# The last three attention chunks in shared runs: one run of sketches, one run of numerators

## The chip, the cores and the metric

The kernel runs on one core of a Trainium2 chip. The metric is the device time of one execution in microseconds (us); lower is better. Five engines work in parallel, each through its own list of instructions in order: TensorE (PE in the profile, its weight loads PEld), VectorE (DVE), ScalarE (ACT), GpSimd (POOL) and SyncE (SP), which issues transfers.

## The reference: what is computed

A sketched attention and an MLP with an exact gelu follow each other. Everything is float32.

```python
# q, k, v: (batch 4, heads 4, 1088 tokens, 32); S1, S2: (8, 32)
phi(x) = outer(S1 @ x, S2 @ x), flattened to 64        # for each token
kv  = sum over tokens of phi(k) x v                    # 64 x 32 for each batch and head
z   = sum over tokens of phi(k)                        # 64
att = (phi(q) @ kv) / (phi(q) @ z + 1e-6)
x   = att as (4352 tokens, 128)                        # heads side by side
h   = x @ w_in                                         # (4352, 2048)
out = (0.5 * h * (1 + erf(h / sqrt(2)))) @ w_out       # (4352, 128)
```

## The kernel before

**Chunks.** The tokens of each batch are cut into two chunks of 512 (`CW`); with four batches that makes `NMAIN` = 8 main chunks, numbered 0 to 7. The last 64 tokens of all four batches together form the remainder, chunk 8 (`NMAIN`), 256 tokens wide. Chunks 2b and 2b + 1 belong to batch b.

**Steps.** The MLP sets the pace. `steps` lists the pairs (chunk, fi), 16 values of fi for each chunk: one step is one block of 128 hidden channels. In each step `hidden` (L692) multiplies the chunk's tokens `xT[n]` by a piece of w_in, ScalarE takes the gelu (L699), and the products with w_out (`two_products`, L776) of earlier steps follow. From chunk 2 on the output product is done with sums of token halves that GpSimd makes (`token_sums`, L741 to L744); `drain` (L791 to L797, with ScalarE's copies L788 and L789) takes its accumulators, and `store` combines, transposes (L838) and sends the result through SP (L853). Chunk n starts at step 16n. The order is written out by hand: `at(t, f)` puts a piece of other work into `slots[t]`, behind the hidden product of step t and ahead of the output products of that step. The last lines tie each engine to the order of the text.

**The attention work in the slots.** For each chunk n from 2 on:

- `query_turn` (L519): VectorE transposes the queries into `qT[n]`.
- `query_sketch` (L568): TensorE multiplies them by `S_abc[b]`, which holds S1, S1 weighted with batch b's z, and S2. The output goes to the first half of each of two PSUM banks.
- `query_outer` (L580 to L603): VectorE transposes the sketch into the other half of the same banks, sums the denominators, takes reciprocals, builds the features divided by them, and transposes those into `qp[n]`.
- `attend` (L617): TensorE multiplies `qp[n]` by `kz[b]`, which gives the numerators, already divided; ScalarE copies them to `xT[n]` (L623).

Between batches there are also, ahead of the first chunk of batch b: `z_sum` (L428 with `k_s` and `ones`), the sum of key features; `fold_z` (L483, L485, L486), in which VectorE weights the sketch with z and writes it into `S_abc[b]`; `kv_sum` (L428 with `k_p` and `v`); `take_kv` (L453), ScalarE's copy of kv to `kv_T[b]`; and `turn_kv` (L458, L459), which turns it into `kz[b]`.

**Runs of small products.** `hidden` and `two_products` use all 128 rows of the array with 64 columns each (128\*64 in the profile). `query_sketch` and `attend` use 64 rows with 32 columns (64\*32), and `kv_product` 128 rows with 32 columns. Where such products follow each other without a hidden product in between, the text calls that a run. Before the change the runs towards the end are, by the step in whose slot they stand:

| step | run |
|---|---|
| 79 | z of batch 3, kv of batch 3, numerators of chunk 5, sketch of chunk 6 |
| 81 | `turn_kv` for batch 3 (128\*64) |
| 95 | numerators of chunk 6, sketch of chunk 7 |
| 111 | numerators of chunk 7, sketch of chunk 8 |
| 127 | numerators of chunk 8 |

Each `query_outer` stands right behind the sketch that it works on. Numerators of a chunk are made in the slot just ahead of its first hidden product.

**Banks.** `work_banks()` gives a tile of two PSUM banks from a pool of two such tiles (`w_ps`). Each of z, kv with numerators, and sketch takes a tile of its own in the run at step 79: `z_sum` a `work_bank()`, `kv_and_attend` a `work_banks()`, `query_sketch` a `work_banks()`. Buffers that matter: `qT`, `q_pT` two each, `xT` three, `q_f` one.

Of the kernel before, what the change touches and what calls it, by code (L numbers as in the profile page):

```python
# [8 lines left out]
FP = mybir.dt.float32  # L9
# [7 lines left out]
def kernel(  # L17
# [21 lines left out]
    F = R * R  # L39
    d_model = out.shape[1]  # L40
    d_ff = moe_w_in.shape[1]
    NF = d_ff // 128
# [5 lines left out]
    CW = JC * 128  # L48
# [4 lines left out]
    NMAIN = B * NCH  # L53
# [7 lines left out]
    att = ctx.enter_context(tc.tile_pool(name="att", bufs=2))  # L61
# [5 lines left out]
    def work_banks():  # L67

        return wps.tile([128, 2, CW], FP, name="w_ps")

    def work_bank():
        return work_banks()[:, 0]
# [159 lines left out]
    ones = big.tile([128, D], FP, name="ones")  # L232
# [173 lines left out]
    k_s = {}  # L406
# [19 lines left out]
    def kv_product(ps, lhsT, features, h, part, start=False, stop=False):  # L426

        pe.matmul(ps[h * D:(h + 1) * D, part * F:(part + 1) * F], lhsT=lhsT, rhs=features, start=start, stop=stop,  # L428
                  skip_group_check=True)

    def kv_sum(b, ps):


        for i in range(J):
            for h in range(H):
                kv_product(ps, main["v", b][:, h, i, :], k_p[b][h // 2][:, i, h % 2], h, 0, start=i == 0)
        for h in range(H):
            kv_product(ps, v_rem_aug[b][:, h, :], flat(k_p_rem[b % 2][:, h]), h, 0, stop=True)

    def z_sum(b):  # L440

        held["z"] = work_bank()
        for h in range(H):
            kv_product(held["z"], ones, k_s[b][:, h], h, 0, start=True, stop=True)

    def fold_z(b):
        sketch_of_z(b, held["z"], 0)
# [3 lines left out]
    def take_kv(b, ps):  # L451
        kv_T[b] = att.tile([128, F], FP, name="kv_T")
        act.copy(out=kv_T[b], in_=ps[:, :F])  # L453

    def turn_kv(b, banks):

        for rows in (slice(0, 64), slice(64, 128)):
            pe.matmul(banks[rows, 1, :128], lhsT=kv_T[b], rhs=ident, start=True, stop=True)  # L458
        act.copy(out=kz[b], in_=banks[:, 1, :128])  # L459
# [48 lines left out]
    qT, qp, xT = {}, {}, {}  # L508
# [15 lines left out]
    def expand_products(n):  # L524


        W = width[n]
        for i in range(2):
            B_of[n, i] = work_banks()
        for s in range(2):  # L530
            for g in range(G):
                for c in range(NP):
                    rows = slice(g * D, (g + 1) * D)
                    pe.matmul(B_of[n, g // 2][c * F:(c + 1) * F, g % 2, s * W // 2:(s + 1) * W // 2],  # L534
                              lhsT=Srep[rows, s].rearrange("p i j -> p (i j)"),
# [7 lines left out]
    def expand_multiply(n, i):  # L543
        W = width[n]
        a, b = (t.rearrange("f g (r x) -> f g r x", r=2) for t in (A[i][:, :, :W // 2], B_of[n, i][:, :, W // 2:W]))
# [8 lines left out]

    sketched = {}

    def query_sketch(n, ps=None):

        ps = work_banks() if ps is None else ps
        W = width[n]  # L560
        m = 1 if n < NMAIN else B // 2
        N = W // 2 // m
        for s in range(2):
            for i in range(m):
                for fh in range(2):
                    for c in range(NP):
                        rows, q4 = slice(c * 64, (c + 1) * 64), 2 * s + fh
                        pe.matmul(ps[q4 * 32:(q4 + 1) * 32, c, i * N:(i + 1) * N],  # L568
                                  lhsT=S_abc[batch_of(n, s, i)][rows, fh].rearrange("p r x -> p (r x)"),
                                  rhs=qT[n].rearrange("p h j t -> p (h j t)")[rows, (s * m + i) * N:(s * m + i + 1) * N],  # L570
                                  start=True, stop=True)
        sketched[n] = ps

    def query_outer(n):

        W = width[n]
        K, H2 = W // 16, W // 2
        ps = sketched.pop(n)
        tok = ps[:, :, CW // 2:CW // 2 + H2]
        dve.transpose(out=tok, in_=ps[:, :, :H2])  # L580
        x = tok.rearrange("p c (k x) -> p c k x", x=2 * R)
        a, b = x[:, :, :, 0:4], x[:, :, :, 8:16]
        m = att.tile([128, 32, 4], FP, name="q_ac")[:, :K]
        den = att.tile([128, 32], FP, name="q_den")[:, :K]
        by_c = lambda t: t.rearrange("p (c k) i -> p c k i", c=NP)
        dve.tensor_copy(out=by_c(m), in_=x[:, :, :, 4:8])
        dve.tensor_mul(out=by_c(m), in0=a, in1=by_c(m))
        part = ps[:, 0, :K]
        dve.tensor_reduce(out=part, in_=m, axis=mybir.AxisListType.X, op=AX.add)
        for g in range(4):  # L590
            dve.tensor_reduce(out=den[(g ^ 1) * 32:((g ^ 1) + 1) * 32], in_=m[g * 32:(g + 1) * 32], axis=mybir.AxisListType.X,
                              op=AX.add)
        dve.scalar_tensor_tensor(out=den, in0=part, scalar=1e-6, in1=den, op0=AX.add, op1=AX.add)
        dve.reciprocal(out=den, in_=den)
        dve.tensor_mul(out=by_c(m), in0=a,
                       in1=den.rearrange("p (c k) -> p c k", c=NP)[:, :, :, None].broadcast_to([128, NP, K // 2, 4]))
        feat = att.tile([128, 2 * CW], FP, name="q_f", bufs=1)[:, :2 * W]
        qp[n] = att.tile([128, 2, CW], FP, name="q_pT")
        for c in range(NP):
            dve.tensor_mul(out=feat[:, c * W:(c + 1) * W].rearrange("p (k i j) -> p k i j", i=4, j=R),  # L600
                           in0=by_c(m)[:, c, :, :, None].broadcast_to([128, K // 2, 4, R]),
                           in1=b[:, c, :, None, :].broadcast_to([128, K // 2, 4, R]))
        dve.transpose(out=qp[n].rearrange("f r x -> f (r x)")[:, :2 * W], in_=feat)  # L603

    def attend(n, banks=None):


        W = width[n]
        m = 1 if n < NMAIN else B // 2
        banks = work_banks() if banks is None else banks  # L610
        f = qp[n].rearrange("f r x -> f (r x)")[:, :2 * W].rearrange("f (c i n r t) -> f c i n r t", c=NP, i=m, r=2, t=32)
        N = W // 2 // m
        for i in range(m):
            for s in range(2):
                rows, b = slice(s * 64, (s + 1) * 64), batch_of(n, s, i)
                for h in range(H):
                    pe.matmul(banks[h * D:(h + 1) * D, s, i * N:(i + 1) * N],  # L617
                              lhsT=(kz[b] if b else kz_first)[rows, h * D:(h + 1) * D],
                              rhs=f[rows, h // 2, i, :, h % 2], start=True, stop=True)
        xT[n] = att.tile([128, CW], FP, name="xT", bufs=3)  # L620
        to = xT[n][:, :W]
        to = to.rearrange("p (s x) -> p s x", s=2) if m == 1 else to.rearrange("p (s t i) -> p s i t", s=2, i=m)
        act.copy(out=to, in_=banks[:, :, :W // 2] if m == 1 else banks[:, :, :W // 2].rearrange("p s (i t) -> p s i t", i=m))  # L623
# [253 lines left out]
    banks = [out_bank(), out_bank()]  # L877
# [59 lines left out]
    def at(t, f, *a):  # L937
        slots[t].append(lambda: f(*a))
# [40 lines left out]
    held = {}  # L979

    def sketch_and_attend(n):
# [2 lines left out]
        query_sketch(n, ps)  # L984
        attend(n - 1, ps[:, :, CW // 2:])

    def turn_keys_rem(pair):
        held["rem"] = work_bank()
        key_turn_rem(pair, held["rem"], by_act)
# [46 lines left out]
    for n in range(3, NCHUNK):  # L1036

        t = (n - 1) * NF
        b = (n + 1) // 2 if n % 2 else n // 2
        keys = n % 2 and b < B  # L1040
        if n > 3:
            at(t - 6, query_turn, n)
        if keys:
            at(t - 1, sketch_and_attend, n)
            at(t - 1, features_of_all, b)
        else:
            if n % 2 == 0 and b < B:
                at(t - 1, z_sum, b)
                at(t - 1, fold_z, b)
                at(t - 1, kv_and_attend, b, n - 1)  # L1050
                at(t + 1, lambda b=b: turn_kv(b, held["kv"]))
            else:
                at(t - 1, attend, n - 1)
            at(t - 1, query_sketch, n)
        at(t - 1, query_outer, n)
        if keys:
            for r in range(2):
                at(t - 3 if n > 3 else t - 4, key_turn_blocks, b, r)

        if n == NMAIN:  # L1060
            at(t + 15, attend, n)
        if keys:
            at(t + 5 + (n == NCH + 1), outer_of_all, b)
            at(t + 5 + (n == NCH + 1), add_tokens, b)
            at(t + 8, widen_v_rem, b)
            if b == 2:
                at(t + 10, turn_first_kv)
# [5 lines left out]
    for t, (n, fi) in enumerate(steps):  # L1073
# [13 lines left out]
        elif fi % NB == NB - 1:  # L1087
            b = fi // NB
# [11 lines left out]
    for t in range(len(steps) + LAG):  # L1100
        if t < 4:
# [9 lines left out]
            if t == 3:  # L1111
                banks = work_banks()
# [23 lines left out]
        if t < len(steps):  # L1136
            n, fi = steps[t]
            hidden(n, fi, by_halves=t >= 18 and (n < NMAIN or fi < 5))
        if t < len(steps) and steps[t][0] < NMAIN and steps[t][1] % NB == NB - 1:
            n, b = steps[t][0], steps[t][1] // NB  # L1140
# [50 lines left out]
```

## Time and profile before

| | us |
|---|---|
| median of 3 runs | 259.96 (259.6 to 260.07) |
| the profiled execution's own time | 259.86 |
| its span, first to last instruction | 258.0 |
| PE busy | 253.8 |
| POOL busy | 163.8 |
| DVE busy | 150.6 |
| ACT busy | 115.0 |
| mean granted TensorE clock | 1.000 |

The span leaves out 1.9 us of the profiled execution's own time. Durations of single instructions come from this one execution. Ends of matmuls are modelled, and a matmul's duration holds its way through the array, so starts say more than durations where matmuls follow each other closely. "Idle before" in brackets is the time in which the engine did nothing ahead of the instruction, and behind it stands who ended it.

### The profile page before, as it was taken

The page shows a single profiled execution, that of the slowest core. Times are in us where ns is not written, and L with a number is a line of the kernel's source. Part 1 is how long each engine was busy: PE and PEld are TensorE (multiplying, and loading weights), DVE is VectorE, ACT ScalarE, POOL GpSimd, SP SyncE. Part 2 cuts the span into 40 slices and gives each one's busy share as a digit, 9 for nine tenths or more (in the row PEclk, how much of TensorE's full clock was granted, in tenths as well). Part 3 has the DMA queues.
Part 4 walks back from the last instruction along what each step waited for, and adds up shares of the span by engine and source line. Part 5 has one row for each costly group of instructions (what it writes and reads, how often), then busy time and mean ns, then how long its engine had stood idle before and what let it go on. Part 6 is the DMA issues. An engine that isn't in the chain of part 4 may idle for free.

```text
span 258.0 us, 5758 instructions
## 1 busy us (share of the span) xinstructions
PE 253.8 (98%) x2331; PEld 134.8 (52%) x2331; DVE 150.6 (58%) x312; ACT 115.0 (45%) x222; POOL 163.8 (63%) x173
## 2 busy tenths in 40 slices
PE   8999999999999999999999999999999999999995
PEld 7856444355444545454444455454445444445794
DVE  2896879969698996580278958530565043600330
ACT  4675767433535333533335334533353335334442
POOL 3504016799968777587758784867778776877200
PEclk9999999999999999999999999999999999999999
DMA  6479748820000101101000020020001100010020
GB/s 203 141 211 366 193 94 216 218 54 10 3 0 15 29 1 23 20 13 31 3 0 3 0 35 9 3 41 0 3 0 24 20 4 0 13 31 0 3 41 20
DMA packets 29594, 13.48 MB, mean 52 GB/s; under 512 B 21888, under 2 KB 27776, under 8 KB 29568
## 3 DMA queue, kind: packets, MB, share of 16 engines
q1 hardware_dynamic: 29392, 13.05, 20.3%
q8 instruction: 18, 0.29, 0.4%
q10 hardware_dynamic: 176, 0.07, 0.1%
q14 instruction: 8, 0.07, 0.1%
HBM read 10.88 MB, written 2.23 MB: 51 GB/s over the span
## 4 chain that ended last, share of the span: by engine, by line
PE 98%; ACT 0%; issue 0%
PE h_ps L692 45%; PE o_ps L776 33%; PE o_ps L827 5%; PE w_ps L824 3%; PE w_ps L428 1%; PE w_ps L859 1%; PE w_ps L617 1%; PE w_ps L568 1%; PE o_ps L417 1%; PE w_ps L534 1%; PE h_ps L706 1%; PE w_ps L947 1%; PE h_ps L333 1%; PE w_ps L635 0%; PE w_ps L333 0%; PE h_ps L373 0%
## 5 line engine op out<-in xcount | busy, mean ns | idle before, releaser
L692 PE MATMUL h_ps<-xT,w_in 128*64 128x512 f32 (+3 forms) x514 | 136.9, 576 | 0.0
L699 ACT ACTIVATE block<-h_ps 128x512 f32<-128x512 f32 (+1 forms) x128 | 73.0, 571 | 118.5 <-PE h_ps L692 118.1
L692 PEld LDWEIGHTS h_ps<-xT,w_in 128*64 128x64 f32 (+1 forms) x514 | 41.9, 142 | 30.6 <-issue 11.6
L776 PE MATMUL o_ps<-block,w_out 128*64 128x256 f32 x224 | 57.5, 379 | 0.0
L741 POOL TENSOR_TENSOR bits_low<-block 128x512 f32<-128x512 f32 x28 | 35.8, 1280 | 27.7 <-ACT block L699 27.7
L776 PEld LDWEIGHTS o_ps<-block,w_out 128*64 128x64 f32 x224 | 30.5, 137 | 38.0 <-issue 27.2
L742 POOL TENSOR_TENSOR bits_a<-block 128x512 f32<-128x512 f32 x28 | 35.8, 1277 | 12.0 <-ACT block L699 12.0
L743 POOL TENSOR_TENSOR bits_e<-bits_a,block 128x512 f32<-128x512 f32 x28 | 36.1, 1289 | 2.2
L744 POOL TENSOR_TENSOR bits_m<-block,bits_e 128x512 f32<-128x512 f32 x28 | 35.8, 1278 | 2.2
L580 DVE STREAM_TRANSPOSE w_ps<-w_ps 128x512 f32<-128x512 f32 (+1 forms) x7 | 4.9, 693 | 42.2 <-PE w_ps L568 29.5
L776 PE MATMUL o_ps<-bits_a,small 128*64 128x256 f32 x112 | 28.8, 379 | 0.0
L776 PE MATMUL o_ps<-block,small 128*64 128x256 f32 x112 | 28.8, 379 | 0.0
L776 PE MATMUL o_ps<-bits_low,small 128*64 128x256 f32 x112 | 28.8, 379 | 0.0
L776 PE MATMUL o_ps<-bits_m,w_out 128*64 128x256 f32 x112 | 28.7, 379 | 0.0
L776 PEld LDWEIGHTS o_ps<-block,small 128*64 128x64 f32 x112 | 15.2, 137 | 17.3 <-issue 10.2
L791 DVE COPY sums<-o_ps 64x256 f32<-64x256 f32 x8 | 3.3, 417 | 35.0 <-PE o_ps L776 35.0
L776 PE MATMUL o_ps<-bits_e,small 128*64 128x256 f32 x112 | 17.2, 384 | 0.0
L827 PE MATMUL o_ps<-g,w_out 128*128 128x512 f32 (+1 forms) x34 | 16.5, 572 | 0.0
L776 PEld LDWEIGHTS o_ps<-bits_m,w_out 128*64 128x64 f32 x112 | 15.3, 137 | 0.0
L776 PEld LDWEIGHTS o_ps<-bits_a,small 128*64 128x64 f32 x112 | 15.2, 137 | 0.0
L776 PEld LDWEIGHTS o_ps<-bits_low,small 128*64 128x64 f32 x112 | 15.2, 137 | 0.0
L776 PEld LDWEIGHTS o_ps<-bits_e,small 128*64 128x64 f32 x112 | 7.5, 136 | 10.5 <-issue 8.2
(182 smaller groups left out, 302.2 us busy)
## 6 DMA issues: line engine op xcount, KB each, us to landing
block<-in_moe_w_in_dram SPq DMA_DIRECT2D x3, 512.0 KB, 6.6
block<-in_moe_w_out_dram SPq DMA_DIRECT2D x3, 512.0 KB, 11.9
k<-in_k_dram SPq DMA_DIRECT2D x12, 128.0 KB, 2.8
v<-in_v_dram SPq DMA_DIRECT2D x12, 128.0 KB, 3.1
q<-in_q_dram SPq DMA_DIRECT2D x24, 64.0 KB, 2.2
out_dram<-oT SPq DMA_DIRECT2D x21, 64.0 KB, 2.2
k<-in_k_dram SPq DMA_DIRECT2D x2, 256.0 KB, 2.9
q<-in_q_dram SPq DMA_DIRECT2D x2, 256.0 KB, 4.0
```

The costliest lines, as they stand in the source:

```text
L333: pe.transpose(ps[:, i * 128:(i + 1) * 128], in_=s, identity=ident)
L580: dve.transpose(out=tok, in_=ps[:, :, :H2])
L692: pe.matmul(ps[rows, :W], lhsT=w[:, rows], rhs=xT[n][:, :W], start=True, stop=True)
L699: act.activation(out=g_of[n, fi][:, :W], in_=ps[:, :W], func=ACT.Gelu)
L741: pool.tensor_sub(out=s[3], in0=a11, in1=a21)
L742: pool.tensor_add(out=s[1], in0=a21, in1=a22)
L743: pool.tensor_sub(out=s[2], in0=s[1], in1=a11)
L744: pool.tensor_sub(out=s[4], in0=a12, in1=s[2])
L776: pe.matmul(acc[n][bank][half * 64:(half + 1) * 64, col:col + HW], lhsT=fixed, rhs=moving, start=opens and e == 0 and name in "4715", stop ...
L791: dve.tensor_copy(out=N[lo, 0, one], in_=a0[lo, one])
L824: pe.matmul(o_of[n][i][:, :128], lhsT=g[:, i * 128:(i + 1) * 128], rhs=w_tile(w_out_sb, fi), start=first, stop=final)
L827: pe.matmul(o_of[n][:, cols], lhsT=w_tile(w_out_sb, fi), rhs=g[:, cols], start=first, stop=final)
```

## The change

The sketches of chunks 6, 7 and 8 are made in one run, in the slot of step 79, behind the kv of batch 3 and the numerators of chunk 5. The numerators of chunks 6, 7 and 8 are made in one run, in the slot of step 95. The runs at steps 111 and 127 fall away. `turn_kv` for batch 3 moves from step 81 to step 91. The queries of all three chunks are transposed in the slot of step 74 (before: 74, 90 and 106). `query_outer` of chunk 8 stands right behind the sketches, that of chunk 6 in the slot of step 86, that of chunk 7 in that of step 89.

To find room in the two tiles, the pieces share them. `first` holds z (bank 0, second half), kv (bank 1, second half), then the sketch of chunk 6 (first halves) and that of chunk 8 (in the second halves, from column 320 on). `other` holds the numerators of chunk 5 (first halves) and the sketch of chunk 7 (second halves). Each `query_outer` is told where to put its transposed sketch (`tok`). In the second run, chunks 6 and 7 use the two halves of one tile, and chunk 8 another tile. The features of chunk 8 get a buffer of their own, `q_pT_rem`.

```diff
+    def z_sum_into(b, ps):
         for h in range(H):
-            kv_product(held["z"], ones, k_s[b][:, h], h, 0, start=True, stop=True)
+            kv_product(ps, ones, k_s[b][:, h], h, 0, start=True, stop=True)
...
-    def query_sketch(n, ps=None):
+    def query_sketch(n, ps=None, tok=None):
 
         ps = work_banks() if ps is None else ps
         W = width[n]
+        tok = ps[:, :, CW // 2:] if tok is None else tok
...
-        sketched[n] = ps
+        sketched[n] = ps, tok
...
-        ps = sketched.pop(n)
-        tok = ps[:, :, CW // 2:CW // 2 + H2]
+        ps, tok = sketched.pop(n)
+        tok = tok[:, :, :H2]
         dve.transpose(out=tok, in_=ps[:, :, :H2])
...
-        qp[n] = att.tile([128, 2, CW], FP, name="q_pT")
+        qp[n] = att.tile([128, 2, W], FP, name="q_pT" if n < NMAIN else "q_pT_rem", bufs=2 if n < NMAIN else 1)
...
+    def last_sketches(b):
+
+        first, other = work_banks(), work_banks()
+        held["z"] = first[:, 0, CW // 2:]
+        z_sum_into(b, held["z"])
+        fold_z(b)
+        kv_sum(b, first[:, 1, CW // 2:])
+        attend(NMAIN - 3, other)
+        take_kv(b, first[:, 1, CW // 2:])
+        query_sketch(NMAIN - 2, first)
+        query_sketch(NMAIN - 1, other[:, :, CW // 2:], other)
+        query_sketch(NMAIN, first[:, :, CW // 2 + F:], other)
+        query_outer(NMAIN)
+
+    def last_attends():
+
+        banks = work_banks()
+        attend(NMAIN - 2, banks)
+        attend(NMAIN - 1, banks[:, :, CW // 2:])
+        attend(NMAIN)
...
+        if n == NMAIN - 2:
+            for m in (n, n + 1, NMAIN):
+                at(t - 6, query_turn, m)
+            at(t - 1, last_sketches, b)
+            for i in range(2):
+                at(t + 6 + 3 * i, query_outer, n + i)
+            at(t + 11, lambda b=b: turn_kv(b, work_banks()))
+            at(t + NF - 1, last_attends)
+        if n >= NMAIN - 2:
+            continue
...
-        if n == NMAIN:
-            at(t + 15, attend, n)
```

More of the change, by code (lines that the diff above doesn't have):

```diff
@@ L985, in sketch_and_attend @@
         attend(n - 1, ps[:, :, CW // 2:])
+    def last_sketches(b):
+        first, other = work_banks(), work_banks()
+        held["z"] = first[:, 0, CW // 2:]
+        z_sum_into(b, held["z"])
+        fold_z(b)
[11 more added lines that the diff above has]
+        attend(NMAIN)
     def turn_keys_rem(pair):
```

## The prediction

> **What bounds the kernel now.** I read the page first: busy times and the chain of work that ended last.
>
> ```profile
> PE 253.8 (98%) x2331; PEld 134.8 (52%) x2331; DVE 150.6 (58%) x312; ACT 115.0 (45%) x222; POOL 163.8 (63%) x173
> ...
> PE 98%; ACT 0%; issue 0%
> ```
>
> TensorE (PE) is busy for 98% of the span and is 98% of the chain; no other engine is above 63%. So what counts is time added to or taken from TensorE's own line, and every moment in which it stands still in the steady part moves the end by as much. I therefore read the timeline around the attention runs. Columns: start, duration, engine, line, operation. First the run ahead of chunk 5, with batch 3's kv:
>
> ```profile
> 153.25 0.32 PE L428 MATMUL w_ps<-k_s,ones 128*32 128x64 f32 x8
> ...
> 153.39 1.08 PE L428 MATMUL w_ps<-k_p,v 128*32 128x64 f32 x64
> 153.64 0.23 DVE L483 TENSOR_TENSOR z_s<-w_ps,sT 128x64 f32<-128x64 f32 x1 [2.34 <-PE w_ps L428]
> 153.90 0.23 DVE L485 TENSOR_REDUCE w_ps<-z_s 128x8 f32<-128x64 f32 x1
> 154.16 0.17 DVE L486 TENSOR_TENSOR S_abc<-w_ps,own_r 128x16 f32<-128x16 f32 x1
> ...
> 154.50 0.66 PE L617 MATMUL w_ps<-q_pT,kz 64*32 64x256 f32 x16
> ...
> 154.96 0.64 PE L568 MATMUL w_ps<-qT,S_abc 64*32 64x256 f32 x16
> 155.27 0.58 ACT L623 COPY xT<-w_ps 128x512 f32<-128x512 f32 x1 [1.31 <-PE w_ps L617]
> 155.53 0.65 PE L776 MATMUL o_ps<-bits_e,small 128*64 128x256 f32 x4
> ...
> 155.76 0.22 ACT L453 COPY kv_T<-w_ps 128x64 f32<-128x64 f32 x1
> 155.91 0.25 PEld L692 LDWEIGHTS h_ps<-xT,w_in 128*64 128x64 f32 x4 [0.19 <-ACT xT L623]
> 156.01 1.03 PE L692 MATMUL h_ps<-xT,w_in 128*64 128x512 f32 x4
> ```
>
> Here TensorE never waits: it goes from z (L428, k_s) to kv at once while VectorE folds z (until 154.33) beside it, and from the numerators (L617) to the sketch (L568) at once while ScalarE copies xT and kv_T (until 155.98) beside it. Then the run ahead of chunk 6, which ends with the sketch of chunk 7:
>
> ```profile
> 180.76 1.03 PE L692 MATMUL h_ps<-xT,w_in 128*64 128x512 f32 x4
> 181.72 0.18 PEld L617 LDWEIGHTS w_ps<-q_pT,kz 64*32 64x32 f32 x16 [0.81 <-issue]
> 181.72 0.66 PE L617 MATMUL w_ps<-q_pT,kz 64*32 64x256 f32 x16
> ...
> 182.17 0.64 PE L568 MATMUL w_ps<-qT,S_abc 64*32 64x256 f32 x16
> 182.49 0.58 ACT L623 COPY xT<-w_ps 128x512 f32<-128x512 f32 x1
> 182.74 0.20 PEld L776 LDWEIGHTS o_ps<-bits_e,small 128*64 128x64 f32 x4 [0.41 <-issue]
> ...
> 183.22 1.03 PE L692 MATMUL h_ps<-xT,w_in 128*64 128x512 f32 x4
> ```
>
> Durations of matmuls include their way through the array, so I work with starts. A step of hidden products takes 0.86 us where the steps follow each other, so the one at 180.76 is issued by 181.62; the run starts 0.10 later. Numerators take 0.45, the sketch 0.43 (the rate of the other 256-column groups), so it is done at 182.60; the next products start 0.14 later, and their four take 0.48 instead of the usual 0.43. A run on 64-row tiles thus costs 0.10 + 0.14 + 0.05 = 0.29 us beside its own products.
>
> **What the Trainium skill says.** "TensorEngine Tiling (Array Packing)", Key Properties: a change of tiling mode drains TensorE. The trace agrees: both gaps stand where 128\*64 turns into 64\*32 and back. "PSUM — Partial Sum Buffer", PSUM bank collisions raise a hardware error: two engines that touch one bank in the same quadrant need an order between them, also at different addresses. The trace before neither shows nor denies it, as TensorE and the reader keep to different tiles there wherever that matters; for waits B and C below it gives the reason. For A it gives none (z and kv lie in the two banks of one tile), and I take the wait from the built program. The same page, Engine vs sequencer instructions: matmuls start and end in program order, so one that waits holds all behind it. "TensorE: Matmul & The Clock Gate", What's actually happening: about 3.4 us of idleness lower the clock. The waits below are near 1 us each; the clock before is 1.00 throughout, and I count nothing for it.
>
> **The change part by part.**
>
> Removed: two runs of their own, ahead of chunks 7 and 8. Their products stay (numerators of chunk 7 and of the remainder, sketches of chunk 7 and of the remainder, at the same size), but ride in runs that exist anyway. Gain 2 x 0.29 = 0.58 us on TensorE, all of it on the path.
>
> Added, wait A: z and kv now lie in one tile, `first`. In the built program kv's first product gains a wait for the last step of `fold_z` (the S_abc write). All of kv's products (64 + 8 rows in the trace), and everything behind them, queue behind it. z's first product starts at 153.25; the fold ends at 154.16 + 0.17 = 154.33. How fast a release is, the run ahead of chunk 2 shows, where TensorE did wait for such a write: L486 ends at 56.04 + 0.17 = 56.21, and L568 starts at 56.36, 0.15 later. So kv starts at 154.48 instead of 153.39: **+1.09**.
>
> Added, wait B: the sketch of chunk 6 goes into `first` too, and waits for ScalarE's copy of kv_T out of it, which is queued behind the copy of chunk 5's xT. Numerators to start of the xT copy 155.27 − 154.50 = 0.77; to the end of kv_T 155.98 − 155.27 = 0.71; release 0.15 (xT ends at 183.07, and L692 starts at 183.22). Together 1.63 after the numerators' start, where the sketch started 0.46 after it: **+1.17**. Behind it stand all three sketches and chunk 5's first hidden step. The sketches of chunks 7 and 8 add no wait.
>
> Added, wait C: ahead of chunk 6 the numerators of chunks 6 and 7 go into halves of one tile, `banks`, and those of chunk 7 wait for the xT copy of chunk 6: 0.77 + 0.58 + 0.15 = 1.50 after the first start instead of 0.45: **+1.05**. The remainder's numerators have a tile of their own and no wait more.
>
> Moved at no cost, and under what cover. Three query transposes now follow each other on VectorE ahead of z (0.71 + 0.45 more): it was idle for 2.34 us before L483, so 1.2 us are left. The remainder's `query_outer` (about 4.4 us, L580 at 209.84 to L603's end at 214.27) follows the sketches at once, in an idle stretch of VectorE before chunk 4's drain. `query_outer` of chunks 6 and 7 follow that drain, 6.4 us each (155.72 to 162.13): with the drain's end 11.8 us after chunk 5's first hidden step (167.78 − 156.01), they end at 18.2 and 24.6, and the numerators start at 25.7. `turn_kv` is later (its two products 0.22 in both places) and needs VectorE's last read of `first`, at 16.9; its place is at 18.9. Chunk 4's combine, transpose and four output DMAs on SP then come some 11 us later than before, and are needed by no one before chunk 5's drain at 35.6; the orders of SP and POOL are unchanged. ScalarE copies xT three times in a row (1.6 us in all) where it has a second of idleness per hidden step; the gelu of chunk 6's first step comes behind them, as its product does. If the cover of the two `query_outer` fails, TensorE waits for VectorE in place of C.
>
> Sum: 1.09 + 1.17 + 1.05 − 0.58 = **+2.73 us** against the profiled execution's own 259.86, which stands 0.10 under the median of the runs: 262.6.
>
> Bounds: the three waits appear nowhere in the trace before. From below each is what the reader alone takes: A 0.23 + 0.23 + 0.17 = 0.63, B 0.58, C 0.58, together 1.8 with no way between the engines, net +1.2. From above, 0.3 more for each release than I take, net +3.6. I take the sums worked out, since each of their terms is a distance seen in this trace. A gain from waiting is excluded: nothing else bounds TensorE here.
>
> **The rivals.**
>
> *Clean merge (faster).* The waits end before TensorE gets there, and only the 0.58 is left: 259.3 us. For it: the order of the text puts work between each pair. Against it: at all three places the work between is none or shorter than the reader's. It decides once the three waits together stay under 0.58 us; one xT copy alone takes that.
>
> *Waits in part covered.* One of them is no stop, or two are half as long: 261.4 us. For it: A and B lie in one run, and a late TensorE may find some of its partners done. Against it: each starts only when the product before it has ended.
>
> *VectorE becomes late.* The two `query_outer` ends come behind the numerators of chunk 7: the cover is 26.2 − 24.6 = 1.6 us, or 2.6 with wait C. If VectorE falls 3.6 us behind there, the end moves by 1 more: 263.6. Against it: the same `query_outer` takes 6.4 us at 155.7 and at 182.9.
>
> **How the numbers follow.** Forecast 0.82, covered in part 0.09, VectorE late 0.06, clean merge 0.03. The time is the forecast's, 262.6. The range 261.4 to 263.5 holds the forecast with an error of about 0.3 for each wait, and reaches to the second case and nearly the third. A measurement can tell 0.2% (0.5 us) from no change: faster 0.03, same 0.02, slower 0.95.
>
> **What would show it right or wrong.** In the timeline after: an idle of about 1.1 us ahead of the first k_p product ended by VectorE, one of about 1.2 ahead of the sketch of chunk 6 ended by ScalarE's kv_T, one of about 1.0 between the numerators of chunks 6 and 7 ended by xT; between the last hidden step of chunks 6 and 7 and the next products no gap; TensorE's busy time nearly unchanged. No idle at those places, or one ahead of numerators ended by VectorE, would prove it wrong.

## The result and the profile after

The changed kernel takes 262.72 us (median of 4 runs, 262.19 to 262.73) against 259.83 us for the kernel before (4 runs, 259.6 to 260.07): a ratio of 1.0101, 95% interval 1.0085 to 1.0117. It is slower by 2.9 us going by the medians, by 2.6 us going by the ratio; the prediction said 262.6 us and slower.

The page of the changed kernel, busy times:

```profile
PE 253.9 (97%) x2331; PEld 135.1 (52%) x2331; DVE 151.0 (58%) x312; ACT 115.1 (44%) x222; POOL 163.5 (63%) x173
```

The span went from 258.0 to 260.9 us and TensorE's busy time stayed (253.8 to 253.9): it does as much as before and stands still longer. The timeline says where. Most line numbers are three or four higher than before (L692 is now L696, L568 L572, L617 L621, L623 L627, L776 L780). The first run, step 79, in the changed kernel (start, duration, engine, line, operation; in brackets the idle before and who ended it):

```profile
153.46 0.32 PE L428 MATMUL w_ps<-k_s,ones 128*32 128x64 f32 x8
...
154.37 0.17 DVE L489 TENSOR_TENSOR S_abc<-w_ps,own_r 128x16 f32<-128x16 f32 x1
...
154.60 1.10 PE L428 MATMUL w_ps<-k_p,v 128*32 128x64 f32 x64 [0.82 <-DVE S_abc L489]
...
155.74 0.66 PE L621 MATMUL w_ps<-q_pT,kz 64*32 64x256 f32 x16
156.51 0.59 ACT L627 COPY xT<-w_ps 128x512 f32<-128x512 f32 x1 [2.34 <-PE w_ps L621]
...
157.00 0.22 ACT L456 COPY kv_T<-w_ps 128x64 f32<-128x64 f32 x1
...
157.27 1.10 PE L572 MATMUL w_ps<-qT,S_abc 64*32 64x256 f32 x32 [0.86 <-ACT kv_T L456]
...
158.16 0.63 PE L572 MATMUL w_ps<-qT_rem,S_abc 64*32 64x64 f32 x32
158.72 0.20 PEld L780 LDWEIGHTS o_ps<-bits_e,small 128*64 128x64 f32 x4
...
159.20 1.03 PE L696 MATMUL h_ps<-xT,w_in 128*64 128x512 f32 x4
```

Waits A and B are there, each ended by the instruction that the prediction named. Read the starts: from z to kv it was 0.14 us (153.25 to 153.39) and is 1.14 (153.46 to 154.60); from the numerators to the sketch it was 0.46 and is 1.53 (155.74 to 157.27). The bracketed idle is smaller than the loss, because it counts only after the modelled end of the matmuls before. Then the second run, step 95:

```profile
183.95 1.03 PE L696 MATMUL h_ps<-xT,w_in 128*64 128x512 f32 x4
...
184.91 0.66 PE L621 MATMUL w_ps<-q_pT,kz 64*32 64x256 f32 x16
...
185.68 0.59 ACT L627 COPY xT<-w_ps 128x512 f32<-128x512 f32 x1
...
186.32 0.67 PE L621 MATMUL w_ps<-q_pT,kz 64*32 64x256 f32 x16 [0.75 <-ACT xT L627]
...
186.77 0.24 PE L621 MATMUL w_ps<-q_pT_rem,kz_first 64*32 64x64 f32 x4
...
187.29 0.20 PEld L780 LDWEIGHTS o_ps<-bits_e,small 128*64 128x64 f32 x4
...
187.77 1.03 PE L696 MATMUL h_ps<-xT,w_in 128*64 128x512 f32 x4
```

Wait C: the numerators of chunk 7 start 1.41 us after those of chunk 6, where 0.45 would do. And where a run fell away, the end of chunk 6:

```profile
212.30 1.03 PE L696 MATMUL h_ps<-xT,w_in 128*64 128x512 f32 x4
...
213.16 0.60 PE L780 MATMUL o_ps<-bits_e,small 128*64 128x256 f32 x4
```

The products follow the hidden step after 0.86 us, with no gap. The table gives the stages around the four places, in us between starts. Each begins with the last hidden product of the chunk before:

| stage | before | after | difference |
|---|---|---|---|
| run ahead of chunk 5 (to its first hidden product) | 3.72 | 6.69 | +2.97 |
| run ahead of chunk 6 | 2.46 | 3.82 | +1.36 |
| ahead of chunk 7 (here no run is left) | 2.47 | 1.29 | −1.18 |
| ahead of chunk 8 (no run left; to the second group of output products) | 1.82 | 1.29 | −0.53 |
| sum | | | **+2.62** |

From the start of the first of these to the last end the traces give the same +2.62 (152.29 to 236.57; 152.51 to 239.41). So nothing is lost or won between these stages. The changed kernel's profile is already 0.2 us later at 31 us, long before anything of the change, which makes up the rest of the spans' 2.9.

### The profile page after: what moved, and what is told of

Read it like the earlier page. It is cut to its first block, busy times and chain, and to the rows that moved or that the text cites. A ratio compares the mean times of both kernels' runs of the same rounds, so it can differ in the third digit from the quotient of the medians.

```text
span 260.9 us, 5759 instructions
## 1 busy us (share of the span) xinstructions
PE 253.9 (97%) x2331; PEld 135.1 (52%) x2331; DVE 151.0 (58%) x312; ACT 115.1 (44%) x222; POOL 163.5 (63%) x173
## 4 chain that ended last, share of the span: by engine, by line
PE 97%; ACT 1%; issue 0%; DVE 0%
PE h_ps L696 44%; PE o_ps L780 33%; PE o_ps L831 5%; PE w_ps L828 3%; PE w_ps L428 2%; PE w_ps L621 1%; PE w_ps L572 1%; PE w_ps L863 1%; PE o_ps L417 1%; PE w_ps L537 1%; PE h_ps L710 1%; PE w_ps L951 1%; PE h_ps L333 0%; ACT xT L627 0%; PE w_ps L639 0%
## 5 line engine op out<-in xcount | busy, mean ns | idle before, releaser
L696 PE MATMUL h_ps<-xT,w_in 128*64 128x512 f32 (+3 forms) x514 | 136.9, 576 | 0.0
L696 PEld LDWEIGHTS h_ps<-xT,w_in 128*64 128x64 f32 (+1 forms) x514 | 41.9, 143 | 30.5 <-issue 11.6
L780 PE MATMUL o_ps<-block,w_out 128*64 128x256 f32 x224 | 57.5, 379 | 0.0
L780 PEld LDWEIGHTS o_ps<-block,w_out 128*64 128x64 f32 x224 | 30.5, 137 | 38.1 <-issue 27.5
L780 PE MATMUL o_ps<-bits_a,small 128*64 128x256 f32 x112 | 28.8, 380 | 0.0
L780 PE MATMUL o_ps<-bits_low,small 128*64 128x256 f32 x112 | 28.8, 380 | 0.0
L780 PE MATMUL o_ps<-block,small 128*64 128x256 f32 x112 | 28.8, 379 | 0.0
L780 PE MATMUL o_ps<-bits_m,w_out 128*64 128x256 f32 x112 | 28.7, 379 | 0.0
L780 PEld LDWEIGHTS o_ps<-block,small 128*64 128x64 f32 x112 | 15.2, 137 | 17.9 <-issue 10.8
L780 PE MATMUL o_ps<-bits_e,small 128*64 128x256 f32 x112 | 17.1, 383 | 0.0
L780 PEld LDWEIGHTS o_ps<-bits_m,w_out 128*64 128x64 f32 x112 | 15.3, 137 | 0.0
L780 PEld LDWEIGHTS o_ps<-bits_a,small 128*64 128x64 f32 x112 | 15.2, 137 | 0.0
L780 PEld LDWEIGHTS o_ps<-bits_low,small 128*64 128x64 f32 x112 | 15.2, 137 | 0.0
L780 PEld LDWEIGHTS o_ps<-bits_e,small 128*64 128x64 f32 x112 | 7.6, 137 | 10.3 <-issue 8.4
```

The source lines that it names most:

```text
L696: pe.matmul(ps[rows, :W], lhsT=w[:, rows], rhs=xT[n][:, :W], start=True, stop=True)
L780: pe.matmul(acc[n][bank][half * 64:(half + 1) * 64, col:col + HW], lhsT=fixed, rhs=moving, start=opens and e == 0 and name in "4715", stop ...
```

## Experiments

The theory: the loss is the three waits, and they come from pieces that share a tile of two banks; the shared runs themselves gain. The rivals: VectorE's new order makes the loss; a run less gains nothing; a lifted wait only moves to the next product. All ratios are to the kernel before on the same chip. For e1 to e4 the us are worked out from the ratio (by it the changed kernel is at +2.6), for e5 to e8 from the medians; the two differ by at most 0.3. "The stretch" is the time in a trace from the first start in the table to the first hidden product behind its last stage.

**e1: z in the other tile.** Wait A alone is lifted.

```diff
-        held["z"] = first[:, 0, CW // 2:]
+        held["z"] = other[:, 0, CW // 2:]
```

> The changed kernel with z in the tile `other` instead of `first`, so that kv shares no tile with what VectorE still reads. If the waits make the loss (theory): wait A, 1.00 us in the trace of the changed kernel, goes and nothing takes its place, since the numerators of chunk 5, which now wait for the fold, start 1.25 us after z and the fold is released 1.14 us after it: 1.0 us under the changed kernel, so about +1.9 us over the kernel before; the first kv product starts 0.14 us after z. If the loss comes from VectorE's new order (rival): nothing changes, +2.9 us. If the run as a whole is late for another reason, the idle moves to the numerators: +2.9 us.

Measured: 261.74 us, ratio 1.0066 (1.0053 to 1.0079), +1.7 us. The trace has kv 0.14 us behind z again:

```profile
153.52 0.32 PE L428 MATMUL w_ps<-k_s,ones 128*32 128x64 f32 x8
...
153.66 1.08 PE L428 MATMUL w_ps<-k_p,v 128*32 128x64 f32 x64
...
154.78 0.66 PE L621 MATMUL w_ps<-q_pT,kz 64*32 64x256 f32 x16
```

The numerators of chunk 5, which now share a tile with z, come 1.26 us after it and don't wait. The stage ahead of chunk 5 takes 5.67 us (152.56 to 158.23), 1.02 less than in the changed kernel. Waits B and C stand as in the changed kernel.

**e2: kv copied first, sketches in the order 6, 8, 7.** Wait B alone.

```diff
+        take_kv(b, first[:, 1, CW // 2:])
         attend(NMAIN - 3, other)
-        take_kv(b, first[:, 1, CW // 2:])
         query_sketch(NMAIN - 2, first)
+        query_sketch(NMAIN, first[:, :, CW // 2 + F:], other)
         query_sketch(NMAIN - 1, other[:, :, CW // 2:], other)
-        query_sketch(NMAIN, first[:, :, CW // 2 + F:], other)
```

> The changed kernel with ScalarE's copy of kv ahead of the numerators of chunk 5, and the sketches in the order 6, 8, 7. Theory: the copy of kv_T is over 0.36 us after the numerators' start, before TensorE comes to the sketch of chunk 6 at 0.46; chunk 8's sketch lies in the same tile and needs no more; chunk 7's waits for the xT copy, over 1.41 us after the numerators' start, where TensorE comes at 1.31: wait B falls from 1.07 to 0.1 us, so about +1.9 us over the kernel before. Rival (ScalarE or VectorE is late as such): the idle stays at about 1 us ahead of some sketch, +2.9 us.

Measured: 261.93 us, ratio 1.0067 (1.0054 to 1.0080), +1.7 us. The timeline of e2, the same columns:

```profile
155.84 0.66 PE L621 MATMUL w_ps<-q_pT,kz 64*32 64x256 f32 x16
156.01 0.21 ACT L456 COPY kv_T<-w_ps 128x64 f32<-128x64 f32 x1 [1.74 <-PE w_ps L428]
...
156.29 0.65 PE L572 MATMUL w_ps<-qT,S_abc 64*32 64x256 f32 x16
...
156.61 0.59 ACT L627 COPY xT<-w_ps 128x512 f32<-128x512 f32 x1 [0.39 <-PE w_ps L621]
156.73 0.64 PE L572 MATMUL w_ps<-qT_rem,S_abc 64*32 64x64 f32 x32
157.25 0.67 PE L572 MATMUL w_ps<-qT,S_abc 64*32 64x256 f32 x16
```

The kv copy now ends (156.22) before TensorE comes to the sketch, and the two sketches that need only it cover the xT copy: 0.52 us from the second to the third sketch instead of 0.42, so 0.10 of wait is left of 1.07.

**e3: the xT copies last.** `attend` is split into its products and its copy; wait C alone.

```diff
-        attend(NMAIN - 2, banks)
-        attend(NMAIN - 1, banks[:, :, CW // 2:])
-        attend(NMAIN)
+        numerators(NMAIN - 2, banks)
+        numerators(NMAIN - 1, banks[:, :, CW // 2:])
+        rest = numerators(NMAIN)
+        take_x(NMAIN - 2, banks)
+        take_x(NMAIN - 1, banks[:, :, CW // 2:])
+        take_x(NMAIN, rest)
```

> The changed kernel with the numerators of chunks 6, 7 and 8 issued first and the three xT copies behind them, so that no product waits for a copy. Theory: wait C (0.96 us) goes; chunk 6's first hidden product needs its xT by about 1.9 us after the run's start, and it is there by 1.9 at the latest: about +1.9 us over the kernel before, at most 0.1 more. Rival (the copy is late for the hidden product instead): the wait moves to the first hidden product of chunk 6 and the time stays at +2.9 us.

Measured: 261.48 us, ratio 1.0057 (1.0044 to 1.0069), +1.5 us (+1.1 to +1.8), a little better than expected; the stage ahead of chunk 6 takes 2.84 us (184.35 to 187.19), 0.98 less than in the changed kernel. In e3's timeline the copies start only behind the products of both chunks in the tile, and still end in time:

```profile
185.31 1.09 PE L624 MATMUL w_ps<-q_pT,kz 64*32 64x256 f32 x32
...
186.51 1.38 ACT L636 COPY xT<-w_ps 128x512 f32<-128x512 f32 x3 [0.49 <-PE w_ps L624]
...
186.71 0.65 PE L789 MATMUL o_ps<-bits_e,small 128*64 128x256 f32 x4
187.15 0.20 PEld L705 LDWEIGHTS h_ps<-xT,w_in 128*64 128x64 f32 x4 [0.24 <-ACT xT L636]
187.19 1.03 PE L705 MATMUL h_ps<-xT,w_in 128*64 128x512 f32 x4
```

**e4: the three edits together.**

> The three edits together (z in the other tile, kv copied first with sketches 6, 8, 7, the xT copies last). Theory: only the gain of two runs less is left, 0.58 us, less 0.1 us of rest wait and 0.14 us that the remainder's numerators take more in the shared run: 0.3 us faster than the kernel before (about 259.5 us). If the shared runs save nothing as such (rival): equal to the kernel before or 0.2 us slower. If the waits are not the whole loss: over 0.5 us slower than before.

Measured: 259.67 us (13 runs) against 259.94 (19 runs), ratio 0.9990 (0.9982 to 0.9998): about 0.3 us faster than the kernel before, near the limit of what can be told. Its stages take 4.70 us ahead of chunk 5 and 2.84 ahead of chunk 6, which with the −1.18 and −0.53 of the two runs less makes +0.98 + 0.38 − 1.71 = −0.35. None of the three waits is left:

```profile
153.82 0.32 PE L428 MATMUL w_ps<-k_s,ones 128*32 128x64 f32 x8
...
153.95 1.08 PE L428 MATMUL w_ps<-k_p,v 128*32 128x64 f32 x64
...
155.07 0.66 PE L624 MATMUL w_ps<-q_pT,kz 64*32 64x256 f32 x16
...
155.53 0.64 PE L572 MATMUL w_ps<-qT,S_abc 64*32 64x256 f32 x16
...
183.26 1.09 PE L624 MATMUL w_ps<-q_pT,kz 64*32 64x256 f32 x32
...
185.15 1.03 PE L705 MATMUL h_ps<-xT,w_in 128*64 128x512 f32 x4
```

e4 keeps every move on VectorE, so its new order costs nothing that shows, and the waits are the whole loss.

**e6: the kernel before with wait A alone, three times.** z shares the tile of kv and numerators in each of batches 1 to 3; nothing else of the change is in it.

```diff
     def z_sum(b):
-        held["z"] = work_bank()
+        held["kv"] = work_banks()
+        held["z"] = held["kv"][:, 0, CW // 2:]
...
-        banks = held["kv"] = work_banks()
+        banks = held["kv"]
```

> The kernel before, with z put into the second half of the first bank of the tile that kv and the numerators use, for batches 1, 2 and 3: wait A three times, with nothing else of the change. Theory: three times 1.00 us, +3.0 us, with an idle of about 0.8 us (1.0 for the weight loads) ahead of kv's first product each time. Rival (the wait only costs where VectorE or the merged run is late): under 1 us.

Measured: 263.30 us, ratio 1.0125 (1.0109 to 1.0141), +3.2 us, 1.06 for each; in its trace kv comes 1.06, 1.01 and 1.00 us later behind z. From its list of waits (total us, times, longest):

```profile
PEld w_ps L428 <- DVE S_abc L487: 3.0, 3, 1.1
PE w_ps L428 <- DVE S_abc L487: 2.5, 3, 0.9
```

z and kv lie in different banks here as in the change. So sharing the tile is enough for the wait; the two need not share a bank.

**e5: one run made into two, in the kernel before, for chunks 6 to 8.** A first try to measure what a run costs.

```diff
-            at(t - 1, query_sketch, n)
-        at(t - 1, query_outer, n)
+            at(t if n > NMAIN - 3 else t - 1, query_sketch, n)
+        at(t if n > NMAIN - 3 else t - 1, query_outer, n)
```

> The kernel before, with the sketches of chunks 6, 7 and 8 (and the feature work behind them) one step later, so that each is a run of its own: three runs more, the same products. Measures what a run costs beside its products. Theory: 3 x 0.29 = 0.87 us, so +0.9 us (0.3%). If a change of tiling costs nothing (rival): 0.

Measured: 261.95 us, ratio 1.0069 (1.0054 to 1.0083), +1.8 us: twice what was expected. The timeline of e5 ahead of chunk 6 says why:

```profile
183.43 0.65 PE L776 MATMUL o_ps<-bits_e,small 128*64 128x256 f32 x4
183.60 0.59 ACT L623 COPY xT<-w_ps 128x512 f32<-128x512 f32 x1
...
184.24 1.08 PE L692 MATMUL h_ps<-xT,w_in 128*64 128x512 f32 x4 [0.16 <-ACT xT L623]
```

The sketch that was moved away had covered the xT copy. Without it the hidden product comes 0.81 us after the products before it instead of 0.48; the same 0.81 stands ahead of chunks 5 and 7. Three times 0.33 and three times 0.29 make 1.86, and the stretch in the trace is 1.91 us longer than in the kernel before. So e5 mixes two costs and does not measure the run by itself; the next two do.

**e7 and e8: six sketches more, together or apart.** Both issue the products of the sketches of chunks 6 and 7 three more times each: e7 in the same run, e8 in six runs of their own.

```diff
+        for i in range(3 if n in (6, 7) and TOGETHER else 0):
+            sketch_products(n, sketched[n])
...
+            for i in range(3 if n in (6, 7) and not TOGETHER else 0):
+                at(t + 6 + 2 * i, sketch_products, n)
```

> The kernel before with the products of the sketches of chunks 6 and 7 issued four times instead of once, the additional ones right behind the first into the same banks: six sketches more, no run more. Both theories: 6 x 0.43 = 2.6 us more than the kernel before.

> The kernel before with the same six additional sketches, each alone in the slot of a step (6, 8 and 10 steps after the chunk's start) into a tile of its own that nobody reads: six runs more. If a run on 64-row tiles costs 0.29 us beside its products (theory): 6 x (0.43 + 0.29) = 4.3 us more than the kernel before, 1.7 more than with the same products together. If the change of tiling costs nothing (rival): 2.6 us, as together.

Measured: e7 262.56 us, ratio 1.0102 (1.0082 to 1.0122), +2.7 us; e8 264.27 us, ratio 1.0167 (1.0147 to 1.0187), +4.4 us. The six runs of their own cost 1.71 us by the medians, 0.285 each. In the traces the stretch is 1.87 us longer in e8 than in e7, 0.31 each. In e8's timeline:

```profile
170.22 1.03 PE L698 MATMUL h_ps<-xT,w_in 128*64 128x512 f32 x4
171.18 0.66 PE L574 MATMUL w_ps<-qT,S_abc 64*32 64x256 f32 x16
171.77 0.43 PE L782 MATMUL o_ps<-block,w_out 128*64 128x256 f32 x1
```

0.96 us for a hidden step that takes 0.86, and 0.59 for a sketch of 0.43: gaps of 0.10 and about 0.15, at each of the six runs as in the kernel before. About 0.05 more goes into the first products behind each.

## Why the prediction was right

- **TensorE bounds, and what stops it moves the end.** Right: the traces' +2.62 us is the sum of the four stages on TensorE. With one wait lifted, the stretch is 1.03, 0.97 and 0.98 us shorter than in the changed kernel (e1, e2, e3), and the whole time follows: +1.7, +1.7 and +1.5 us where the changed kernel has +2.6.
- **Wait A, +1.09.** Measured +1.00 in the changed kernel, 1.06 for each in e6. It ended with the S_abc write, as named. e1 and e6 show that the shared tile makes it.
- **Wait B, +1.17.** Measured +1.07. The chain was right: numerators, xT copy, kv_T copy, sketch. e2 shows that it is ScalarE's order: the copy of kv stood behind one that it doesn't need.
- **Wait C, +1.05.** Measured +0.96, and gone in e3.
- **The term that was mis-sized in all three: the release of 0.15 us.** It is 0.06 in A (154.54 to 154.60), 0.05 in B (157.22 to 157.27) and 0.05 in C (186.27 to 186.32). Neither of the two places it was read from shows a release alone. Ahead of chunk 2 the sketch also changes the tiling, and TensorE hardly had to wait:

```profile
56.04 0.17 DVE L486 TENSOR_TENSOR S_abc<-w_ps,own_r 128x16 f32<-128x16 f32 x1
56.09 0.29 PE L428 MATMUL w_ps<-k_p_rem,v_rem_aug 128*32 128x64 f32 x8
...
56.36 0.67 PE L568 MATMUL w_ps<-qT,S_abc 64*32 64x256 f32 x16
```

From kv's last products to the sketch it is 0.27 us; at the same place in e6, where the fold is over long before, it is 0.23 (57.51 to 57.74). And the hidden product at 183.22 stands 0.48 us behind the products before it, as it does in the changed kernel (158.72 to 159.20), where xT was long done: it did not wait for xT either. Together the three terms are about 0.3 us too large.
- **Two runs less, −0.58.** The 0.29 for a run was right (0.285 by the medians of e7 and e8, 0.31 by their traces). What came out is 2.62 − 3.03 = −0.41, since the remainder's numerators take 0.38 us in the shared run (186.77 to the gap of 0.14 ahead of 187.29) and took about 0.24 in a run of their own (235.70 to the same gap ahead of 236.09). From the kernel before:

```profile
235.70 0.26 PE L617 MATMUL w_ps<-q_pT,kz_first 64*32 64x64 f32 x4
...
236.09 0.65 PE L776 MATMUL o_ps<-bits_e,small 128*64 128x256 f32 x4
```

The prediction had them at the same size. This error and that of the release point opposite ways. That the sum is only 0.1 off in the trace is in part luck: the release alone would have left it off by about 0.3, still inside the range.
- **Moves at no cost.** Right: VectorE waits 0.97 us for z (predicted slack 1.2), its features for chunk 7 end at 183.49, 24.3 us after chunk 5's first hidden product (predicted 24.6), before their numerators at 186.3. (The "second" of ScalarE's idleness per hidden step is 1.1 us.) And e4 keeps all of this and loses nothing that shows.
- **The rivals.** The clean merge, put at 259.3 us, is what e4 comes near to (259.67) once the waits are lifted. So the idea behind the change holds, but its gain (0.3 us) is a tenth of what this form of it loses.

The Trainium skill, "TensorEngine Tiling (Array Packing)", Key Properties, says that a change of tiling mode drains TensorE, without a price; the price of a run in and out is about 0.3 us here. That the drain is what takes it is not shown: weight loads and products start together behind such a change (181.72 for both in the kernel before), and no run takes the two apart. The idle of about 1 us left the granted clock at 0.999, as executions of the kernel before have it (0.998 to 1.000).

## What to carry to other kernels

Where one engine is the bound and others read what it writes, work placed between write and reuse is the cover of the reader; putting pieces into one tile to save a run takes that cover away, and each reader then costs its whole chain (here about 1 us each). Before merging, list for each tile who reads it between two writes; let the reader that is needed first go first, put pieces with no reader in between into the same tile, and issue products ahead of the copies that they don't need. A merged run is worth little (about 0.3 us here), one exposed chain more than three times that.

## What was not expected of the hardware

A release from VectorE or ScalarE to a waiting TensorE shows as 0.05 to 0.06 us between the end of the one and the start of the other: at the three waits of the changed kernel, and in e5 (184.19 to 184.24). In the one place where the tiling changes too it was 0.15 (56.21 to 56.36).

Thirty-two rows of 64-column products took about 0.25 us in a run of their own and about 0.4 behind 256-column products of the same tiling. The remainder's numerators took 0.24 and 0.38. Its sketch took 0.42 in the kernel before (209.17 to 209.73, less the gap of 0.14), behind numerators of 256 columns; in e5, where it is a run of its own, it took 0.25 (0.41 less a gap of about 0.16):

```profile
212.94 0.48 PE L568 MATMUL w_ps<-qT_rem,S_abc 64*32 64x64 f32 x32
213.35 0.43 PE L776 MATMUL o_ps<-block,w_out 128*64 128x256 f32 x1
```

Why, no run here tells.
